# Three chained layers on one core: where TensorE's idle products write, how far they go on, and from which gap they are put in

## The chip, the cores and the metric

The kernel runs on one core of one Trainium2 chip. The metric is the device time of one execution in microseconds (us), lower is better. TensorE (PE) multiplies matrices, VectorE (DVE), ScalarE (ACT) and GpSimd (POOL) work on elements, SyncE (SP) issues most transfers. All five take their own instructions in order and wait for each other by semaphores.

## The reference, cut to what matters

Three layers follow each other. Everything is float32; 4 batches of 576 tokens, 512 columns.

```
attention: softmax(mask(q k^T / 8)) v         8 heads of 64, window of 64 tokens
channel mix: xk = mu_k x + (1-mu_k) x_prev ;  xr likewise with mu_r
             sigmoid(xr w_r) * (max(xk w_k, 0)^2 w_v)
gated conv:  (sigmoid(conv5(x)) * (x w_val)) w_out
```

## The kernel before, in words

The 2304 tokens are cut into a first block of 256 and four of 512. Of each block, attention is computed in four units of two heads (`unit`, units 0 to 3 are the first block, 4 to 7 the second). A unit's steps are: scores on PE (`qk`, L416; its masking products stand in L423 and L427, the products of q and k in L433), row maxima on DVE (`top`, L468 and the line before), exponentials on ACT (`exp`, L476), a division by the row sum on DVE (`norm`, L486), transposes on PE (`tp`, L491 to L497), a copy of the transposed weights to SBUF by ACT or DVE (`pt`, L503 to L505), the product with the values on PE (`pv`, L508 to L512), and a copy of its result into `xT` by DVE or ACT (`x`, L517 to L519). `xT` feeds the channel mix, whose first product is an `r` product (`r_tile`, L627 in the first block).

Which instruction stands where is a table written by hand (`SLOT`): each step has a number, and `Plan.run` issues the steps in that order. `Plan.run` also keeps a rough forecast of when each step can start. Where a PE step is forecast to start more than `WAIT` after the PE step ahead of it, `Plan.run` calls `fill`, which puts in idle products: 128x128 products of a zeroed tile (`warm`, part of `sgs`) whose result no one reads. Their number is the forecast gap divided by `PASS`.

PSUM has three users in the opening. `p0` holds the scores of units 0 to 3 (two buffers). `scores` holds those of the later units; before, the idle products write there, so they have to end when unit 4's scores are made. `at` has two banks: transposes write the first; in the first block the value product of a unit writes the first 256 columns of the second bank, which `x` then reads. The other 256 columns of that bank are not used in the first block.

```
if w[0] == "pe" and self.fill and t - free.get("pe", self.BEGIN) > self.WAIT:
    self.fill(t, int((t - max(free.get("pe", 0), self.WARM) - 250) // self.PASS))
```

Of the kernel before, what the change touches and what calls it, by code (L numbers as in the profile page):

```python
# [8 lines left out]
F32 = mybir.dt.float32  # L9
# [11 lines left out]
P = 128  # L21
# [3 lines left out]
TA = 256  # L25
HP = H // 2
NF = DM // P
NFF = DFF // P
GAP = TAPS - 1
TB = 512  # L30
# [143 lines left out]
class Plan:  # L174
# [2 lines left out]
    TO_PE = 110  # L177
    BEGIN, START, LAND = 740, 700, 1270
    RAMP, STALL = 3500, 1300
    WAIT, PASS, WARM = 700, 430, 900  # L180
    TABLE = 1280

    def __init__(self, **rings):
# [2 lines left out]
    def op(self, key, eng, ns, deps, fn, ring=None, table=None, moves=0):  # L186

        self.ops.append((key, ((eng, ns, fn),), deps, ring, table, moves))

    def any(self, key, deps, *ways):  # L190

        self.ops.append((key, ways, deps, None, None, 0))
# [45 lines left out]
def tile_kernel(ctx, tc, qkh, vh, mu, conv, w_k, w_v, w_r, w_val, w_out, out):  # L238
    nc = tc.nc
    f32 = lambda ap: ap.bitcast(F32)  # L240
    V, G, ACT, PE, DMA = nc.vector, nc.gpsimd, nc.scalar, nc.tensor, nc.sync
# [49 lines left out]
    pq = pas.enter_context(tc.tile_pool(name="pq", bufs=1, space=PSUM, side="right"))  # L291
    pa = pas.enter_context(tc.tile_pool(name="pa", bufs=1, space=PSUM, side="right"))
# [3 lines left out]
    Q = {}  # L296
# [4 lines left out]
    warm = sgs[:, 0, :P]  # L301
# [68 lines left out]
    A = {}  # L370
# [3 lines left out]
    def unit(u):  # L374

        t, hp = UNITS[u]
        t0, n = BLOCKS[t]
# [62 lines left out]
        scores = lambda: a["ps"].rearrange("p h (c j) -> p h c j", j=P)[:, :, :n2]  # L440
# [48 lines left out]
        at = lambda b: Q["at"][:, b]  # L489

        def tp():  # L491
            if "at" not in Q:
                Q["at"] = pa.tile([P, 2, TB], F32, tag="at", name="at")
            a["pt"] = tile_(mx, "pt", [P, 2, TB])
            for i in range(2 * n2):
                b, c = divmod(i, n2) if t else (0, i)
                PE.transpose(at(b)[:, c * P:(c + 1) * P], a["s"][:, i, :], ident)  # L497
        op(("tp", u), "pe", 176 * n2 + 2, [("norm", u), "ident", *back("pv", 1), *([("x", w) for w in range(HP)] if t == 1 else [])], tp,
           ring=("pa", ("pts", u)))
        for h in range(2 if t else 1):  # L500
            pts = lambda h=h: (a["pt"][:, h, :n], at(h)[:, :n]) if t else (a["pt"][:, :, :n], at(0).rearrange("p (h q) -> p h q", h=2))
            m = n if t else 2 * n
# [102 lines left out]
    Ps, Sg, Ss, Rk = {}, {}, {}, {}  # L605
# [425 lines left out]
    for i, (key, w, dst, nm) in enumerate(pieces):  # L1031
        m = nm * key[1]
        users[key] = []
        for e in range(nm // P):
            k = (dict(w_r="r", w_k="h", w_v="v")[key[0]], m // P + e)
# [109 lines left out]

    idle = {}

    def first_idle():  # L1150
        idle["ps"] = Q["scores"] = pq.tile([P, 2, TB], F32, tag="qk", name="scores")
    op("idle", "none", 0, ["warm"], first_idle)

    def fill(t, n):
        if any(k in Ps for k in [("r", 0, m) for m in range(NF)]) or HP in A and "ps" in A[HP] or n <= 0:
            return
        for _ in range(n):
            PE.matmul(idle["ps"][:, 0, :P], lhsT=warm, rhs=warm, start=True, stop=True)
    plan.fill = fill
    with tc.manual_schedule():  # L1160
        plan.run()
# [52 lines left out]
```

## Time and profile before

| | |
|---|---|
| Runs shown | 421.28, 422.95, 423.63 us; median 422.95 |
| The profiled execution: own time, span | 423.3 us, 421.5 us |
| PE busy | 410.9 us, 97% of the span |
| DVE, ACT, POOL busy | 351.9, 256.7, 22.5 us |
| Idle products | 11, on line L1158 |

A busy PE is counted from modelled ends of matmuls. A float32 product shows as two matmul records. The times below are from the span's start.

### The profile page before, as it was taken

Reading aid. Unit: us, or ns where it says so; the run is one execution under the profiler, and the core shown is the slowest. Engines: PE = TensorE matmul, PEld = TensorE weight load, DVE = VectorE, ACT = ScalarE, POOL = GpSimd, SP = SyncE. Lnnn points to the kernel's source line nnn. Section 1 sums busy time; section 2 is a strip of 40 time slices with the busy share of each in tenths; the row PEclk is TensorE's granted clock in tenths of the full one; section 3 lists DMA queues with packets and bytes.
Section 4 is the critical chain, followed back from the end, with each engine's and each line's share of the span. In section 5 each row is a group of like instructions: output and inputs, shape, how many; then the busy total and the mean of one; then the engine's idle time right before and its main releaser. Section 6 shows DMA issues by size and latency. Waiting matters only on the chain.

```text
span 421.5 us, 9145 instructions
## 1 busy us (share of the span) xinstructions
PE 410.9 (97%) x3746; PEld 354.8 (84%) x3746; DVE 351.9 (83%) x511; ACT 256.7 (61%) x585; POOL 22.5 (5%) x62
## 2 busy tenths in 40 slices
PE   8789999999999999999999999999999999999996
PEld 6578888888888888888888888888888899999996
DVE  3899998988989799458978996988584999999970
ACT  4899997789996175765334645154223284577721
POOL 2114101000002000000000000000000000001000
PEclk9899999999999999999999999999999999999999
DMA  8998925333432522072375434434997913616622
GB/s 306 407 366 320 381 64 166 104 117 104 131 113 98 208 103 77 2 286 89 116 261 210 137 157 155 161 152 153 343 427 286 400 69 114 225 35 155 176 86 112
DMA packets 24714, 77.69 MB, mean 184 GB/s; under 512 B 2528, under 2 KB 3296, under 8 KB 22624
## 3 DMA queue, kind: packets, MB, share of 16 engines
q1 hardware_dynamic: 23952, 74.74, 48.5%
q0 software_dynamic: 576, 2.36, 2.9%
q8 instruction: 29, 0.48, 0.4%
q14 instruction: 13, 0.11, 0.1%
q10 hardware_dynamic: 144, 0.00, 0.0%
HBM read 53.90 MB, written 20.84 MB: 177 GB/s over the span
## 4 chain that ended last, share of the span: by engine, by line
PE 83%; DVE 13%; issue 1%; ACT 1%; ACTq 0%; POOL 0%; DVEq 0%; POOLq 0%
PE h L603 21%; PE v L603 21%; PE r L603 10%; PE at L497 4%; PE ao L512 4%; PE scores L433 4%; PE v L627 3%; PE h L627 3%; PE out L979 3%; PE out2m L873 3%; DVE x L771 2%; DVE gq L771 2%; PE val3m L873 2%; PE r L627 2%; DVE early L914 1%; DVE xt L761 1%
## 5 line engine op out<-in xcount | busy, mean ns | idle before, releaser
L603 PE MATMUL h<-x,wk 128*128 128x512 f32 x384 | 90.7, 391 | 0.0
L603 PEld LDWEIGHTS h<-x,wk 128*128 128x128 f32 x384 | 71.5, 188 | 14.8
L603 PE MATMUL v<-sh,wv 128*128 128x512 f32 x256 | 81.1, 390 | 0.0
L603 PEld LDWEIGHTS v<-sh,wv 128*128 128x128 f32 x256 | 48.1, 188 | 10.0
L603 PE MATMUL v<-sl,wv 128*128 128x512 f32 x128 | 49.8, 389 | 0.0
L603 PE MATMUL r<-x,wr 128*128 128x512 f32 x192 | 45.4, 391 | 0.0
L603 PEld LDWEIGHTS r<-x,wr 128*128 128x128 f32 x192 | 35.7, 188 | 7.3
L804 DVE SCALAR_TENSOR_TENSOR early<-early,wc 128x576 f32<-128x576 f32 x48 | 38.2, 810 | 3.1 <-ACT early L802 2.7
L476 ACT ACTIVATE s<-s,m 128x128 f32<-128x128 f32 x96 | 37.2, 397 | 4.6 <-DVE m L465 4.6
L603 PEld LDWEIGHTS v<-sl,wv 128*128 128x128 f32 x128 | 24.0, 188 | 4.9
L504 ACT ACTIVATE pt<-at 128x512 f32<-128x512 f32 x28 | 16.4, 601 | 13.6 <-PE at L497 13.6
L654 ACT ACTIVATE rk<-h 128x512 f32<-128x512 f32 (+1 forms) x23 | 12.1, 538 | 17.9 <-PE h L603 15.8
L563 DVE SCALAR_TENSOR_TENSOR xm<-xT,omu,xm 128x512 f32<-128x512 f32 x32 | 22.5, 744 | 0.6 <-POOL xT L569 0.6
L684 DVE TENSOR_TENSOR sl<-rk,sh 128x1024 fp32r<-128x1024 f32 x16 | 19.4, 1219 | 3.9 <-ACT rk L682 3.8
L706 DVE TENSOR_TENSOR sgs<-v,sgs 128x512 f32<-128x512 f32 (+1 forms) x20 | 12.5, 632 | 10.9 <-PE v L603 10.9
L678 ACT ACTIVATE sh<-rk 128x1024 fp32r<-128x1024 f32 x16 | 16.9, 1055 | 6.8 <-DVE rk L656 6.7
L512 PEld LDWEIGHTS ao<-pt,vt 128*64 128x64 f32 x512 | 16.2, 138 | 5.5 <-issue 2.8
L586 DVE TENSOR_TENSOR x<-xm,x 128x1024 fp32r<-128x1024 f32 x16 | 19.4, 1219 | 1.2 <-ACT x L583 1.1
L486 DVE TENSOR_TENSOR s<-s,m 128x1024 f32<-128x1024 f32 x16 | 19.5, 1219 | 0.2
L768 ACT ACTIVATE x<-xt 128x576 fp32r<-128x576 f32 x15 | 10.0, 677 | 15.4 <-DVE xt L761 9.4
L476 ACT ACTIVATION_READ_ACCUMULATOR s<-s,m 128x1 f32 x96 | 18.8, 196 | 0.0
L512 PE MATMUL ao<-pt,vt 128*64 128x64 f32 x512 | 18.4, 225 | 0.0
(200 smaller groups left out, 857.5 us busy)
## 6 DMA issues: line engine op xcount, KB each, us to landing
qk<-qk SPq DMA_DIRECT2D x16, 544.0 KB, 5.2
vt<-vh SPq DMA_DIRECT2D x16, 512.0 KB, 4.9
xb<-x2d SPq DMA_DIRECT2D x4, 1152.0 KB, 7.2
out_t<-st SPq DMA_DIRECT2D x15, 288.0 KB, 2.8
x2d<-sgs SPq DMA_DIRECT2D x16, 256.0 KB, 3.5
w_out<-w SPq DMA_DIRECT2D x8, 512.0 KB, 3.5
w_val<-w SPq DMA_DIRECT2D x8, 448.0 KB, 4.5
wk<-w_val SPq DMA_DIRECT2D x2, 1792.0 KB, 11.8
```

Of the source, the lines that this page charges most:

```text
L433: PE.matmul(a["ps"][rows, h, o:o + W + HW], lhsT=a["q"][heads[h], c * HW:(c + 1) * HW], rhs=a["k"][heads[h], c * HW:c * HW + W + HW], star ...
L476: ACT.activation(out=s, in_=scores()[:, c // n2, c % n2, :] if by_pe else s, func=AF.Exp, scale=D ** -0.5 if by_pe else 1.0, bias=l(0)[:, ...
L486: lambda: V.tensor_tensor(out=a["s"], in0=a["s"], in1=l(1).unsqueeze(2).to_broadcast(sq), op=ALU.mult))
L512: PE.matmul(a["o"][heads[h], c * W:(c + 1) * W], lhsT=a["v"][:, c, heads[h]], rhs=a["pt"][:, h, c * W:(c + 1) * W], start=True, stop=True)
L563: V.scalar_tensor_tensor(out=m, in0=xT[:, f, :n], scalar=omu[:, c:c + 1], in1=m, op0=ALU.mult, op1=ALU.add)
L586: lambda E: E.tensor_tensor(out=dst(1), in0=src(), in1=f32(dst(0)), op=ALU.subtract))
L603: PE.matmul(ps, lhsT=a, rhs=b[:, kt, :], start=(kt == 0 and i == 0), stop=(kt == nk - 1 and i == 2))
L627: PE.matmul(Ps[key][:, :n], lhsT=ws(kt), rhs=x()[:, kt, :], start=kt == 0, stop=kt == nk - 1)
L678: ACT.activation(out=Ss[t][0][:, f, :n], in_=rk(), func=AF.Square)
L684: lambda E: E.tensor_tensor(out=Ss[t][1][:, f, :n], in0=rk(), in1=f32(Ss[t][0][:, f, :n]), op=ALU.subtract))
L804: V.scalar_tensor_tensor(out=o, in0=x, scalar=c, in1=o, op0=ALU.mult, op1=ALU.add)
L873: PE.matmul(z[bank][:, j, :HS], lhsT=lhs, rhs=rhs, start=new and kt == 0 and e == 0, stop=kt == 1 and e == 2, skip_group_check=not new)
```

## The change

The idle products get a new place to write, columns 256 to 383 of the second bank of `at`, which is therefore taken from its pool at the start. They no longer end with unit 4's scores: they go on until a unit of the second block has its transposes or an `r` product was issued, whichever is first. `WAIT` goes from 700 to 400 and `PASS` from 430 to 250, so shorter forecast gaps get idle products, and more of them. No row of the order table changes.

```diff
-    WAIT, PASS, WARM = 700, 430, 900
+    WAIT, PASS, WARM = 400, 250, 900
...
         def tp():
-            if "at" not in Q:
-                Q["at"] = pa.tile([P, 2, TB], F32, tag="at", name="at")
             a["pt"] = tile_(mx, "pt", [P, 2, TB])
...
-    idle = {}
-
     def first_idle():
-        idle["ps"] = Q["scores"] = pq.tile([P, 2, TB], F32, tag="qk", name="scores")
+        Q["scores"] = pq.tile([P, 2, TB], F32, tag="qk", name="scores")
+        Q["at"] = pa.tile([P, 2, TB], F32, tag="at", name="at")
...
     def fill(t, n):
-        if any(k in Ps for k in [("r", 0, m) for m in range(NF)]) or HP in A and "ps" in A[HP] or n <= 0:
+        if any(k in Ps for k in [("r", 0, m) for m in range(NF)]) or any("pt" in A[u] for u in A if u >= HP) or n <= 0:
             return
         for _ in range(n):
-            PE.matmul(idle["ps"][:, 0, :P], lhsT=warm, rhs=warm, start=True, stop=True)
+            PE.matmul(Q["at"][:, 1, TA:TA + P], lhsT=warm, rhs=warm, start=True, stop=True)
```

On PE, 11 idle products become 27: 6, 4 and 1 ahead of the first, third and fourth group of scores become 11, 6 and 2, and 1, 2, 3 and 2 are new, ahead of the first transposes and of the first, second and fourth value product. The other four engines issue the same instructions in the same order. In the changed kernel the idle products are on L1155, the transposes on L495, the value products on L510.

PE's first rows, before (`scores` and `qk_160` are PSUM tiles, `one` and `low` the masks that DVE makes):

```order
L1158 MATMUL scores<-sgs 128x128 [waits Pool_49]
L1158 MATMUL scores<-sgs 128x128 x5
L423 LDWEIGHTS one [waits DVE_49]
L423 MATMUL qk_160<-low,one 64x256
L427 LDWEIGHTS one
```

The same rows in the changed kernel:

```order
L1155 MATMUL at<-sgs 128x128 [waits Pool_49]
L1155 MATMUL at<-sgs 128x128 x10
L423 LDWEIGHTS one [waits DVE_49]
L423 MATMUL qk_166<-low,one 64x256
L427 LDWEIGHTS one
```

Five more idle products stand between the start and the first scores; nothing else moved there.

PE from the end of unit 4's scores to unit 2's transposes, before (`xm` and `sgs` on the right hold the weights and values of the first block, `pt_340` and `pt_379` are the transposed weights of units 0 and 1):

```order
L433 MATMUL scores<-qk_148 32x96 x31
L497 MATMUL at<-ident,xm 128x128 [waits DVE_49,Pool_49]
L497 MATMUL at<-ident,xm 128x128 x3
L512 MATMUL at<-pt_340,sgs 64x64 [waits DMAHW0_49,Activation_49]
L512 MATMUL at<-pt_340,sgs 64x64 x7
L497 MATMUL at<-ident,xm 128x128 [waits DVE_49]
L497 MATMUL at<-ident,xm 128x128 x3
L512 MATMUL at<-pt_379,sgs 64x64 [waits DMAHW4_49,DVE_49]
L512 MATMUL at<-pt_379,sgs 64x64 x7
L497 MATMUL at<-ident,xm 128x128 x4
```

The same stretch in the changed kernel:

```order
L433 MATMUL scores<-qk_149 32x96 x31
L1155 MATMUL at<-sgs 128x128
L495 MATMUL at<-ident,xm 128x128 [waits DVE_49,Pool_49]
L495 MATMUL at<-ident,xm 128x128 x3
L1155 MATMUL at<-sgs 128x128 [waits Activation_49]
L1155 MATMUL at<-sgs 128x128
L510 MATMUL at<-pt_349,sgs 64x64 [waits DMAHW0_49]
L510 MATMUL at<-pt_349,sgs 64x64 x7
L495 MATMUL at<-ident,xm 128x128 [waits DVE_49]
L495 MATMUL at<-ident,xm 128x128 x3
L1155 MATMUL at<-sgs 128x128 [waits DVE_49]
L1155 MATMUL at<-sgs 128x128 x2
```

One idle product without a wait of its own comes ahead of the first transposes. The two and the three ahead of the value products now carry the wait for ACT or DVE that the value product carried before; the value product behind them keeps the wait for its transfer alone. The two ahead of the fourth value product stand in the same way.

## Rows read from the trace of the kernel before

**Rows 1.** The page: PE's granted clock in 40 slices of the span.

```profile
PEclk9899999999999999999999999999999999999999
```

**Rows 2.** PE's waits over the span: waited for, us in total, times, longest.

```profile
PE at L512 <- DVE xT L518: 1.2, 1, 1.2
PE at L512 <- DVE pt L505: 1.2, 1, 1.2
...
PE val0m L873 <- ACT early L885: 0.7, 1, 0.7
...
PE at L512 <- ACT pt L504: 0.7, 1, 0.7
```

**Rows 3.** Timeline of PE, the opening: start, us, what [idle before <-releaser].

```profile
0.99 2.93 PE L1158 MATMUL scores<-sgs 128*128 128x128 f32 x12 [0.99 <-POOL sgs L302]
3.85 0.43 PE L423 MATMUL qk<-low,one 64*64 64x256 bf16 x4
...
4.26 0.89 PE L433 MATMUL qk<-early 64*32 64x96 f32 x32
...
5.49 0.74 PE L433 MATMUL qk<-early 64*32 64x96 f32 x32
6.16 1.16 PE L1158 MATMUL scores<-sgs 128*128 128x128 f32 x8
7.81 0.31 PE L423 MATMUL qk<-low,one 64*64 64x256 bf16 x4 [0.49 <-ACT xm L476]
...
8.07 0.56 PE L433 MATMUL qk<-early 64*32 64x96 f32 x32
8.56 0.49 PE L1158 MATMUL scores<-sgs 128*128 128x128 f32 x2
9.20 0.31 PE L423 MATMUL qk<-low,one 64*64 64x256 bf16 x4 [0.16 <-ACT xm L476]
```

**Rows 4.** Timeline of PE, from unit 4's scores to the first `r` product.

```profile
11.82 0.53 PE L433 MATMUL scores<-qk 64*32 64x96 f32 x21 [0.71 <-issue]
12.27 0.66 PE L497 MATMUL at<-ident,xm 128*128 128x128 f32 x4
13.62 0.69 PE L512 MATMUL at<-pt,sgs 128*64 128x64 f32 x16 [0.69 <-ACT pt L504]
...
16.07 1.05 PE L512 MATMUL at<-pt,sgs 128*64 128x64 f32 x16 [1.18 <-DVE pt L505]
17.05 1.12 PE L497 MATMUL at<-ident,xm 128*128 128x128 f32 x4
...
18.73 1.33 PE L433 MATMUL scores<-qk 64*32 64x96 f32 x64
...
22.46 0.69 PE L512 MATMUL at<-pt,rk 128*64 128x64 f32 x16 [1.20 <-DVE xT L518]
23.08 1.13 PE L627 MATMUL r<-x,words 128*128 128x256 f32 x4
```

**Rows 5.** Timeline of PE, scores of unit 6.

```profile
26.25 1.00 PE L433 MATMUL scores<-qk 64*32 64x96 f32 x64
```

**Rows 6.** Timeline of ACT: unit 0's first exponential, a copy of unit 1, a copy of unit 3.

```profile
6.25 0.37 ACT L476 ACTIVATE xm<-qk,first_m 128x128 f32<-128x128 f32 x1 [3.59 <-DVE first_m L468]
...
18.21 0.39 ACT L519 ACTIVATE xT<-at 128x256 f32<-128x256 f32 x1 [0.69 <-PE at L497]
...
21.35 0.60 ACT L504 ACTIVATE pt<-at 128x512 f32<-128x512 f32 x1 [0.44 <-PE at L497]
```

**Rows 7.** Timeline of DVE: the last piece of the masks.

```profile
2.99 0.16 DVE L320 CAST one<-ident 128x128 bf16<-128x128 f32 x1
```

**Rows 8.** The idle products' line: duration ns of one record, min/median/max.

```profile
L1158 PE MATMUL scores<-sgs x22: 275/421/582, 1.0 to 8.8; 128*128 128x128 f32 x22
```

**Rows 9.** Stretches: us, PE, PEld, DVE, ACT, POOL, PEclk, DMA share, GB/s.

```profile
12.93:16.07 3.14, 1.27 (x21) 0.97 (x21) 2.74 (x9) 3.10 (x11) 0.00 (x0) 1.00 1.03 405
17.00:18.00 1.00, 1.00 (x8) 0.72 (x4) 1.00 (x2) 0.52 (x4) 0.51 (x1) 0.50 1.01 420
```

## Prediction, made before the changed kernel ran

> **What bounds the kernel now.** I read the page first, for who is busy and how the clock runs. PE is the engine that is nearly always busy, and its clock is at the upper level (9 is the highest digit) everywhere but in the second of the 40 slices [rows 1]. PE's waits say where PE stands still: 1.2, 1.2 and 0.7 us ahead of the value products on L512, all before the first `r` product, and after it nothing longer than 0.7 us [rows 2]. From 23.08 us, where the first `r` product starts [rows 4], PE feeds itself to the end almost without a gap. So the start of that product decides: what the change moves there, it moves at the end, one for one. It touches nothing later.
>
> The opening is a chain through three engines. PE makes idle products from 0.99 us, then the first scores, whose last group of records ends at 4.26 + 0.89 = 5.15 [rows 3]. ACT, idle for 3.59 us, starts its exponentials at 6.25 [rows 6], and all that follows hangs on them. Further on, transposes (PE), a copy (ACT or DVE) and value products (PE) alternate, and PE stands ahead of each value product until the copy is done [rows 4].
>
> The clock column says 1.00 for the first microseconds, but the work says otherwise: a record of an idle product takes 421 ns in the middle of the list and 275 at best [rows 8], and the q-k records of a score group take 0.89, then 0.74, then 0.56 us [rows 3]. I read this as PE at the lower level until about 6 us, then at the upper one. A second low stretch is in the clock column itself, 0.50 between 17 and 18 us; ahead of it PE had worked 1.27 of 3.14 us [rows 9]. There the 16 records of a value product take 1.05 us instead of 0.69, four transposes 1.12 instead of 0.66 [rows 4].
>
> **The change, part by part.** The price of an idle product first. The twelve records of the first six last 2.93 us, the first alone 0.58, so the other eleven come every (2.93 - 0.58) / 11 = 0.214 us, 0.427 a product, at the low clock. Eight records last 1.16 us and two 0.49, so six more cost 0.67: 0.112 a record, 0.223 a product, at the high clock [rows 3, 8].
>
> Start, 11 products for 6. The masks are ready at 2.99 + 0.16 = 3.15 us [rows 7], and PE comes to the first scores at 3.85 without a gap [rows 3]: the idle products already end last there, so five more push the scores back by 5 x 0.427 = 2.13, to 5.98. What comes then runs at the high clock and takes what the third group takes, 8.07 + 0.56 - 7.81 = 0.82, and ends at 6.80 instead of 5.15. **Delay 1.65.** Bounds: 1.1 if the clock rises while the longer list still runs and the five cost the high price, 2.13 if it rises only after the first scores. I take 1.65, since the present rise, near 6 us, falls just at the new end of the list. ACT's exponentials come later by the same.
>
> Ahead of the third score group, 6 for 4: PE was idle for 0.49 there, waiting for an exponential that also comes later now [rows 3]; two more cost 0.45 and fit. **0**, up to 0.2 if they don't quite. Ahead of the fourth, 2 for 1: the gap was 0.16 [rows 3], the product costs 0.223. **0.06**, between 0 and 0.22.
>
> Ahead of the first transposes, one new product that waits for nothing: PE came there late, straight from unit 4's scores [rows 4]. **0.22**; 0 if the norm ends last there.
>
> Ahead of the first, second and fourth value product, 2, 3 and 2 new ones. The order says what they do: they write a tile that a copy reads, so the wait of the value product has moved to the first idle product ahead of it. PE stands still as long as before, until ACT or DVE is done, and only then makes the idle products, with the value product queued behind them. They lie on the path in full: 7 x 0.223 = **1.56**. Bounds: 0 if the value product's transfer ended last and they hid behind it, 7 x 0.427 = 2.99 at the low clock. Who waits for these products: the next transposes on PE itself, then the `pt` and `x` copies on ACT and DVE.
>
> Here the Trainium skill, page "PSUM — Partial Sum Buffer", section "PSUM bank collisions raise a hardware error", speaks against the change: PSUM is to be guarded by bank and quadrant, not by address, so columns that nobody uses in a bank that is being read are not free. By that rule the three and the last two have to wait, because the second bank is being read, but the first two don't, because the copy ahead of them reads the first bank; the late products would then be five, 1.12 us. In the order of the changed program all three groups carry a wait for ACT or DVE; no run here shows yet which of them costs.
>
> The 0.71 us gap in the middle of unit 4's scores waits for nothing that the profile shows [rows 4]. If something comes in by its own time there, a later PE waits less. Bounds 0 and -0.71; I take **-0.2**, nearer to 0, as the place may hold the gap and not the time.
>
> The low clock after 16 us. In the new order seven products lie between these gaps that PE did not have before, so I expect the clock to stay up. What it gives back on PE: 1.05 - 0.69 = 0.36 on the value product, 1.12 - 0.66 = 0.46 on the transposes [rows 4], 1.33 - 1.00 = 0.33 on the scores of unit 5 [rows 4, 5], 1.15 together. What can pass through: ACT waited 0.69 and 0.44 us for these transposes [rows 6], 1.13. I take **-1.1**, between 0 (it falls all the same) and -1.15.
>
> Other engines' instructions and queues are unchanged; they have the same work behind a later PE, which gives them more time. **0**.
>
> **Sum:** 1.65 + 0 + 0.06 + 0.22 + 1.56 - 0.2 - 1.1 = 2.19, say **+2.3**, since the 0 ahead of the third scores can only err upwards. The profiled execution's own time is 423.3 (span 421.5 and 1.8 around it), which lies 0.35 above the median of the runs, 422.95. 423.3 + 2.3 = 425.6; from the median 425.25. I forecast **425.3 us**.
>
> **The rivals.**
> *A, the clock falls all the same.* The gaps ahead of the copies stay as long as they were, because the idle products stand behind the wait and not in it; nothing in the rows shows that a little work between them is enough. Then -1.1 is gone, and some late products run at the low price: 423.3 + 2.19 + 1.1 = 426.6, up to 427.2. For it: PE had worked through much of the time before the fall and it came nevertheless [rows 9]. Chance 0.22.
> *B, not slower: the clock rises early in the list.* Place: the start. If the longer unbroken stream brings the high clock before 5 us, the five products cost 1.1 and the score groups behind them run fast from their first record; with the unexplained gap swallowed whole and the second fall gone it is 1.1 + 1.56 - 0.71 - 1.1 = 0.85: 424.1, or 423.8 from the median. It decides from a first-score delay of 1.1 or less. Against it: before, PE was as unbroken from 0.99 us on, and the clock came near 6 [rows 3]. The same time comes out if the opening is as I say and the late products hide behind the transfers: 2.19 - 1.56 = 0.6. Chance 0.22.
> In the Trainium skill, page "TensorE: Matmul & The Clock Gate", section "What's actually happening", the throttled state is the default and activity releases it. By that rule alone the added products could only help the clock; it is B's mechanism and the -1.1 of the forecast, and the low records at the start agree with it.
> *C, faster.* B's opening and free late products together: 0.85 - 1.56 = -0.7, 422.6, still no measurable gain. Beyond that I find no source: 0.03.
>
> **How the numbers follow.** A measurement of this kernel tells about 0.5% from no change, 2.1 us: above 425.06 is slower, below 420.84 faster. The forecast has 0.53, and its own range, 424.2 to 426.4, lies about two thirds above the line: 0.35 slower, 0.18 same. A gives 0.22 slower, B 0.22 same, C 0.03 faster: slower 0.57, same 0.40, faster 0.03. For 8 in 10 the range runs from 423.3, inside B, to 427.2, the upper end of A.
>
> **What would show it.** In the new profile: 22 records at the start, the first scores near 6.0 and ACT's first exponential near 7.9 us; idle products directly ahead of three value products, with PE's wait ended by ACT or DVE named at them; no low clock between 16 and 20 us; the first `r` product near 25.3. I am wrong if that product starts before 24 us, if the idle products lie inside the gaps, or if the time after it changes by more than 0.5 us.

## The result, and the profile after

The changed kernel takes 425.56 us (median of 7 executions, 424.99 to 426.3), the kernel before 422.06 (7 executions, 421.28 to 423.63; the three shown ahead are among them). The ratio is 1.0078, 95% interval 1.0059 to 1.0096: 3.5 us slower. The forecast of 425.3 and its range held, and so did its sign. The change itself was forecast as 2.35 us and measured as 3.5; the section on the prediction says by what luck the time came out right all the same.

The profiled execution has an own time of 425.44 us and a span of 423.7. Of the page, the line of PE's granted clock (before: [rows 1]):

```profile
PEclk9999999999999999999999999999999999999999
```

The low slice of before is gone. PE's waits (before: [rows 2]):

```profile
PE at L1155 <- DVE xT L516: 1.2, 1, 1.2
PE at L1155 <- DVE pt L503: 1.2, 1, 1.2
...
PE val0m L871 <- ACT early L883: 0.7, 1, 0.7
PE at L1155 <- ACT pt L502: 0.7, 1, 0.7
PE scores L433 <- issue: 0.4, 1, 0.4
PE qk L423 <- ACT xm L476: 0.4, 1, 0.4
```

The three waits of 1.2, 1.2 and 0.7 us are as long as they were, and they now stand at L1155, the idle products, instead of at the value products (L512 then, L510 now). The timeline of PE in the opening (before: [rows 3]):

```profile
0.99 4.69 PE L1155 MATMUL at<-sgs 128*128 128x128 f32 x22 [0.99 <-POOL sgs L302]
5.61 0.31 PE L423 MATMUL qk<-low,one 64*64 64x256 bf16 x4
...
5.87 0.56 PE L433 MATMUL qk<-early 64*32 64x96 f32 x32
...
7.11 1.60 PE L1155 MATMUL at<-sgs 128*128 128x128 f32 x12
9.09 0.31 PE L423 MATMUL qk<-low,one 64*64 64x256 bf16 x4 [0.37 <-ACT xm L476]
...
10.48 0.31 PE L423 MATMUL qk<-low,one 64*64 64x256 bf16 x4
```

There are 22 records at the start for 12, and the first scores begin at 5.61 for 3.85. Their q-k records take 0.56 us, which is the high clock, where before they took 0.89. ACT's first exponential (before: [rows 6]):

```profile
7.53 0.37 ACT L476 ACTIVATE xm<-qk,first_m 128x128 f32<-128x128 f32 x1 [4.87 <-DVE first_m L468]
```

It is 1.28 us later than before (6.25). PE from unit 4's scores to the first `r` product (before: [rows 4]):

```profile
12.58 0.74 PE L433 MATMUL scores<-qk 64*32 64x96 f32 x37 [0.43 <-issue]
13.24 0.49 PE L1155 MATMUL at<-sgs 128*128 128x128 f32 x2
13.57 0.60 PE L495 MATMUL at<-ident,xm 128*128 128x128 f32 x4
14.86 0.71 PE L1155 MATMUL at<-sgs 128*128 128x128 f32 x4 [0.69 <-ACT pt L502]
15.50 0.69 PE L510 MATMUL at<-pt,sgs 128*64 128x64 f32 x16
...
17.95 0.94 PE L1155 MATMUL at<-sgs 128*128 128x128 f32 x6 [1.18 <-DVE pt L503]
18.82 0.69 PE L510 MATMUL at<-pt,sgs 128*64 128x64 f32 x16
...
20.39 1.00 PE L433 MATMUL scores<-qk 64*32 64x96 f32 x64
...
23.83 0.71 PE L1155 MATMUL at<-sgs 128*128 128x128 f32 x4 [1.24 <-DVE xT L516]
24.47 0.69 PE L510 MATMUL at<-pt,rk 128*64 128x64 f32 x16
25.09 2.00 PE L625 MATMUL r<-x,words 128*128 128x256 f32 x8
```

Each late group begins only when its wait ends, and the value product comes 0.64, 0.87 and 0.64 us behind the group's start. The second group waits for DVE's `pt` copy, which reads the first bank, and not for the `x` copy of the second bank, which is done 0.6 us earlier. Timeline of DVE:

```profile
16.87 0.42 DVE L516 COPY xT<-at 128x256 f32<-128x256 f32 x1 [1.17 <-PE at L495]
17.21 0.68 DVE L503 COPY pt<-at 128x512 f32<-128x512 f32 x1
```

In the forecast's first reading everything depends on the first `r` product, and that holds: from its start to the own time there are 423.3 - 23.08 = 400.22 us before and 425.44 - 25.09 = 400.35 now. In all fourteen profiles of this study this rest lies between 400.1 and 400.5 us, so from here on the start of that product stands for the time of a kernel's profiled execution.

### The profile page after: what moved, and what is told of

Its sections match the earlier page's. It is cut to its first block, busy times and chain, and to the rows that moved or that the text cites. A ratio compares the mean times of both kernels' runs of the same rounds, so it can differ in the third digit from the quotient of the medians.

```text
span 423.7 us, 9206 instructions
## 1 busy us (share of the span) xinstructions
PE 413.6 (98%) x3778; PEld 357.9 (84%) x3778; DVE 351.9 (83%) x511; ACT 257.0 (61%) x585; POOL 21.8 (5%) x62
## 4 chain that ended last, share of the span: by engine, by line
PE 84%; DVE 12%; ACT 1%; issue 1%; ACTq 0%; POOL 0%; DVEq 0%; POOLq 0%
PE h L601 21%; PE v L601 21%; PE r L601 10%; PE ao L510 4%; PE at L495 4%; PE scores L433 3%; PE v L625 3%; PE h L625 3%; PE out L977 3%; PE out2m L871 3%; DVE x L769 2%; DVE gq L769 2%; PE val3m L871 2%; PE at L1155 2%; PE val0m L871 2%; PE r L625 2%
## 5 line engine op out<-in xcount | busy, mean ns | idle before, releaser
L510 PEld LDWEIGHTS ao<-pt,vt 128*64 128x64 f32 x512 | 16.2, 138 | 5.5 <-issue 2.8
L510 PE MATMUL ao<-pt,vt 128*64 128x64 f32 x512 | 18.4, 225 | 0.0
```

The source lines that it names most:

```text
L510: PE.matmul(a["o"][heads[h], c * W:(c + 1) * W], lhsT=a["v"][:, c, heads[h]], rhs=a["pt"][:, h, c * W:(c + 1) * W], start=True, stop=True)
```

## The experiments

All kernels below compute the whole reference and differ in idle products alone (those with bfloat16 products also zero a small tile for them on POOL). Their numbers stand in a table by step instead of coming from the forecast of the plan: (start, third score group, fourth score group) and, ahead of value products, (first, second, fourth). So the kernel before is 6, 4, 1. A "+x" is the median against that of the kernel before in the same set of runs (422.07 for the first four kernels, 35 executions; 422.32 for the next four, 11; 422.35 for the last four, 35). The ratio and its interval go by all executions of both kernels, so they do not give quite the same difference as the medians.

### The added products of the opening alone

```diff
+    IDLE = {('qk', 1): 11, ('qk', 2): 6, ('qk', 3): 2}
```

> The opening alone: 11, 6 and 2 idle products ahead of the first, third and fourth score group, none further on, so PE does the same as the kernel before from unit 4's scores on. Theory (the longer list delays the first scores, the rest of the loss is the products behind the waits): the first exponential on ACT starts near 7.5 us as in the changed kernel, against 6.25 before; the unexplained PE gap shrinks by about 0.3; the time lies 1.0 to 1.3 us above the kernel before. Rival (the opening is absorbed further on, all of the loss is the late products): within 0.4 us of the kernel before. Rival (the opening makes the whole loss): 3 us or more above.

Measured: 423.38 us (422.75 to 424.19), ratio 1.0022, interval 1.0000 to 1.0043: +1.31. Timeline of PE:

```profile
5.50 0.31 PE L423 MATMUL qk<-low,one 64*64 64x256 bf16 x4
...
12.31 0.73 PE L433 MATMUL scores<-qk 64*32 64x96 f32 x37 [0.28 <-issue]
...
22.56 1.99 PE L625 MATMUL r<-x,words 128*128 128x256 f32 x8
```

ACT's first exponential starts at 7.42 us here, 1.17 later than before. By the medians the opening is a third to two fifths of the whole loss; the interval reaches from nothing to half of it. The profiled execution has the lowest time of the twelve (422.75), and its first `r` product is only 0.72 us later than in the second profile of before shown below (22.56 for 21.84), because the stop in unit 4's scores is 0.28 us long in it and not 0.70.

### The late products alone

```diff
+    IDLE = {('qk', 1): 6, ('qk', 2): 4, ('qk', 3): 1, ('pv', 0): 2, ('pv', 1): 3, ('pv', 3): 2}
```

> The late products alone: 6, 4 and 1 at the start as before, and 2, 3 and 2 ahead of the first, second and fourth value product, in the shared tile. Theory: they run after the wait and cost 0.64 + 0.87 + 0.64 = 2.15 us on the path (the starts in the changed kernel's trace); the clock stays up through 20 us; the time lies 1.5 to 2.2 us above the kernel before. Rival (priced by the issue rate alone, 7 x 0.223 = 1.56, and a low clock saved in every execution): 0.5 us above. Rival (the clock falls all the same): 2.2 us or more above, with 0.50 in the clock column.

Measured: 424.16 us (423.5 to 426.52), ratio 1.0044, interval 1.0024 to 1.0065: +2.09. Timeline of PE:

```profile
13.89 0.71 PE L1158 MATMUL at<-sgs 128*128 128x128 f32 x4 [0.69 <-ACT pt L502]
14.54 0.69 PE L510 MATMUL at<-pt,sgs 128*64 128x64 f32 x16
...
16.99 0.94 PE L1158 MATMUL at<-sgs 128*128 128x128 f32 x6 [1.18 <-DVE pt L503]
17.86 0.69 PE L510 MATMUL at<-pt,sgs 128*64 128x64 f32 x16
```

The same waits of 0.69 and 1.18 us end at the idle products, and 0.65 and 0.87 us of idle products follow. The larger part of the loss is here. 1.31 + 2.09 = 3.4, beside 3.5 for the change as a whole.

### The same late products, written where nothing is read

Is it the seven products or their waits that cost? The pool of the second block's value products (`ao`) holds a PSUM bank that nothing uses this early. The late products write there; the opening stays at 6, 4, 1.

```diff
+        Q["spare"] = Q["po"].tile([P, TB], F32, tag="ao", name="spare")
...
+        o = Q["spare"][:, :P] if key[0] == "pv" else Q["at"][:, 1, TA:TA + P]
```

> As the run with the late products alone, but they write to the PSUM bank that the second block's value products use later, which nobody reads yet, so they wait for no copy. Theory (they cost because they stand behind the wait): the value products start as in the kernel before or up to 0.2 us later each, the clock stays up, and the time equals the better executions of the kernel before, 421.3 to 422.1. Rival (the products cost wherever they stand): 1.5 us or more above the kernel before. Rival (the clock was of no importance): within 0.3 us of the kernel before's median, and executions with a low stretch not slower than those without.

Measured: 422.61 us (422.36 to 423.56), ratio 1.0015, interval 0.9996 to 1.0034: +0.54 where the same products behind waits cost 2.09. Timeline of PE:

```profile
13.04 0.61 PE L1159 MATMUL spare<-sgs 128*128 128x128 f32 x4
13.89 0.69 PE L510 MATMUL at<-pt,sgs 128*64 128x64 f32 x16 [0.24 <-ACT pt L502]
...
16.35 0.69 PE L510 MATMUL at<-pt,sgs 128*64 128x64 f32 x16 [0.51 <-DVE pt L503]
...
18.13 1.41 PE L433 MATMUL scores<-qk 64*32 64x96 f32 x64
...
21.94 0.69 PE L510 MATMUL at<-pt,rk 128*64 128x64 f32 x16 [0.76 <-DVE xT L516]
22.55 1.99 PE L626 MATMUL r<-x,words 128*128 128x256 f32 x8
```

The products run at once, inside the gaps, and PE's waits shrink to 0.24, 0.51 and 0.76 us. From the first to the second value product there are 16.35 - 13.89 = 2.46 us, as before without any idle product (16.07 - 13.62 = 2.45 [rows 4]): they cost nothing there. So the waits are the price. The time expected was 421.3 to 422.1, and it is half a microsecond more. In the profile the first `r` product comes 0.71 us later than in the second profile of before (22.55 for 21.84), from two places: the stop in unit 4's scores is 0.98 us for 0.70, and the scores of unit 5 take 1.41 us for 1.00, with a stop of 0.33 us in them that waits for nothing shown (the last section comes back to it).

### The whole change, with its late products in the spare bank

The edit is that of the kernel above, made to the changed kernel: 11, 6, 2, one ahead of the first transposes, and 2, 3, 2 into the spare bank.

> The changed kernel with one thing undone: the products ahead of the value products write to the bank nobody reads, so they fall into the gap. Theory: the changed kernel's time less 2.15, near 423.4, and 1.0 to 1.5 above the kernel before, the opening alone being left. Rival (the opening makes the whole loss): near 425.5. Rival (the late products make the whole loss): at the kernel before's time, near 422.1.

Measured: 423.62 us (423.15 to 424.78), ratio 1.0038, interval 1.0019 to 1.0056: +1.55. That is 1.94 us less than the change as it was made, by the place of seven products alone; what stays is the opening.

### The kernel before, looked at once more

The forecast booked 1.1 us for the low clock after 16 us. This run is the kernel before, unchanged.

> The kernel before, looked at once more. In the five traces so far the time is the start of the first r product plus 400.2 us, and its executions spread from 421.2 to 423.3. Theory (the first profiled execution, 423.3, had a low stretch at 16 to 19.6 us that most executions don't have): this one, if it has no 0.50 stretch, starts the first r product near 21.9 and takes 421.3 to 422.4. Rival (every execution has the low stretch, and the first profile was no exception): a 0.50 stretch before 22 us, and a first r product near 23.

Measured: 422.06 us. Timeline of PE:

```profile
16.06 0.69 PE L512 MATMUL at<-pt,sgs 128*64 128x64 f32 x16 [1.18 <-DVE pt L505]
16.68 0.66 PE L497 MATMUL at<-ident,xm 128*128 128x128 f32 x4
...
17.83 1.00 PE L433 MATMUL scores<-qk 64*32 64x96 f32 x64
...
21.23 0.69 PE L512 MATMUL at<-pt,rk 128*64 128x64 f32 x16 [1.21 <-DVE xT L518]
21.84 1.99 PE L627 MATMUL r<-x,words 128*128 128x256 f32 x8
```

There is no low clock here: the value product takes 0.69, not 1.05 us, the scores 1.00, not 1.33 [rows 4]. The first five rows of the table below agree within 0.01 us in the two executions, and at the first `r` product they differ by 23.08 - 21.84 = 1.24. So the low stretch is an event of some executions and not of others.

How many have it can be read from the mean granted clock that is on record for each execution: it is 0.996 or less in the profiles with a low stretch in the middle and 0.998 or more in those without. Of the 35 executions of the kernel before in the first set, 7 have 0.996 or less; they take 423.02 to 426.16 us. The other 28 have a median of 421.82. In the other two sets it is 2 of 11 and 11 of 35, so 20 of 81 in all. All seven executions of the changed kernel have 0.998 or more. The change does take the low stretch away, but three executions of the kernel before in four have none.

With the second profile as the base, the loss can be read off step by step:

| start, us | before, first profile | before, second | after | after - second |
|---|---|---|---|---|
| first scores | 3.85 | 3.85 | 5.61 | 1.76 |
| third score group | 7.81 | 7.82 | 9.09 | 1.27 |
| first transposes | 12.27 | 12.27 | 13.57 | 1.30 |
| first value product | 13.62 | 13.61 | 15.50 | 1.89 |
| second value product | 16.07 | 16.06 | 18.82 | 2.76 |
| q-k products of unit 5's scores | 18.73 | 17.83 | 20.39 | 2.56 |
| fourth value product | 22.46 | 21.23 | 24.47 | 3.24 |
| first `r` product | 23.08 | 21.84 | 25.09 | 3.25 |

Ahead of the first transposes 1.3 us are lost; then each late group adds its step, 0.59, 0.87 and 0.68, and 0.20 come back ahead of unit 5's scores.

### Shorter idle products: fewer, longer records

A bfloat16 product of 128x512 shows as 2 records (a weight load and a matmul) where a float32 product shows as 4, and takes about as long. If PE's stop in unit 4's scores stands at a count of instructions, such a list moves it. First with the numbers of before (6, 4, 1), then with 4 at the start, then with 4 at the start and 2, 4, 4 such products in the spare bank:

```diff
+            PE.matmul(o.rearrange("p (c j) -> p c j", j=P), lhsT=zero[:, :P],
+                      rhs=zero[:, None, :P].to_broadcast([P, TB // P, P]), start=True, stop=True)
```

> The kernel before with each idle product made as one bf16 product of 128x512 instead of a float32 one of 128x128: the same 0.43 us at the low clock, but two records on PE (one weight load, one product) instead of four, 22 fewer in all; counts 6, 4 and 1, in the second bank of the shared tile. In all six traces PE's unexplained gap stands ahead of its 449th record, 0.5 to 1.2 us long, at 10.9 to 11.9 us, whatever the products. Theory (PE runs out of instructions there, and the gap is tied to the place in the list): the gap stands ahead of record 449 again, now 22 records further on in the work, and is 0.2 to 0.4 us shorter; the time is 0.2 to 0.5 us below the kernel before. Rival (tied to a time or a transfer): the gap stays at the same scores and ends at the same time; time as before.

> As the run with the short list, with 4 products at the start instead of 6. The masks are ready at 3.15 us and the first q-k input lands at 3.67. Theory (the opening is bound by the idle list, as with 11 products): the first scores' masking products start near 3.2 instead of 3.85, the q-k products near 3.75 instead of 4.26, and the time is 0.4 to 0.6 us below the run with 6. Rival (fewer products bring the high clock later, and the first score groups lose what the start gains): no difference, or more.

> As the run with 4 short products at the start, with 2, 4 and 4 more ahead of the first, second and fourth value product, in the bank nobody reads, 20 records. Theory: they fall into the gaps and keep the clock up in every execution, at no cost; the median as in the run with 4, the spread of the executions smaller. Rival (each adds 0.1 to 0.2 to the value product behind it and moves PE's next run-out into the scores of unit 5, as with the float32 products in the gap): 0.3 to 0.6 us above the run with 4.

Measured: 427.02 us (ratio 1.0112, interval 1.0096 to 1.0128), 426.01 (1.0068, 1.0042 to 1.0095) and 424.08 (1.0043, 1.0028 to 1.0059). All are slower than before. The first was expected 0.2 to 0.5 us below the kernel before and lies 4.7 above it. The second lies 1.0 below the first, where 0.4 to 0.6 was expected; the third lies 1.9 below the second, where no difference was. Timeline of PE and the clock line of the page, of the first:

```profile
10.15 0.91 PE L438 MATMUL scores<-qk 64*32 64x96 f32 x54
13.88 0.55 PE L438 MATMUL scores<-qk 64*32 64x96 f32 x10 [2.82 <-issue]
14.36 1.11 PE L500 MATMUL at<-ident,xm 128*128 128x128 f32 x4
...
26.92 1.35 PE L630 MATMUL r<-x,words 128*128 128x256 f32 x5
```

```profile
PEclk9689999999999999999999999999999999999999
```

The stop moved in place, as a count of instructions would have it (54 of the 64 records are done, 43 before), but it grew to 2.82 us, and the low clock followed it (0.50 from 13.78 to 24.02 us). All four executions of the first kernel have a mean clock of 0.988 or less, and four of the six of the second have 0.992 or less. In the third kernel the stop is 1.71 us:

```profile
13.34 0.37 PE L438 MATMUL scores<-qk 64*32 64x96 f32 x8 [1.71 <-issue]
```

The clock stayed up behind it in the profile, but not in every execution as was expected: three of the six have a mean clock of 0.994 to 0.996, and they are the three slowest (424.49 to 424.78). The executions lie within 1.4 us of each other (423.41 to 424.78); in the second kernel they spread over 3.5.

### One product less, and many small ones

The last four look for a version that beats both kernels: 5, 4, 1 in float32; then bfloat16 products of 128x128, four times as many as a float32 list of the same length: 24, 12, 4; 20, 12, 4; and 20, 12, 4 with 2, 4, 4 products of 128x512 in the spare bank.

```diff
+    IDLE = {('qk', 1): 20, ('qk', 2): 12, ('qk', 3): 4, ('pv', 0): 2, ('pv', 1): 4, ('pv', 3): 4}
```

> Before, with 5 idle products at the start instead of 6, everything else as before. If the list at the start is on the path one for one, the first scores come 0.43 us earlier (near 3.4) and the first r product up to 0.4 earlier: 0 to 0.4 us faster than before. If PE's stop ahead of its 449th record is set by the number of records ahead of it, there are 4 records fewer and the stop is 0.1 to 0.2 us longer, which leaves 0.2 to 0.3. Rival: the stop, or the later rise of the clock, takes all of it, and the time is that of before or longer.

> Before, with bfloat16 idle products of 128x128 (2 records each where a float32 product has 4): 24, 12 and 4 ahead of the first, third and fourth score group instead of 6, 4 and 1, so about the same PE time and some 36 records more ahead of the stop in unit 4's scores. If the stop is tied to the 449th record and is shorter where PE comes to it later with more records behind it, it is 0.2 to 0.5 us instead of 0.7 to 1.0, and the time 0.2 to 0.5 us below before. Rival: the stop depends on when PE gets there alone, is as long as before, and the time is the same.

> As the kernel with 24, 12 and 4 bfloat16 idle products, with 20 at the start: the first scores come 4 products, some 0.4 us, earlier. If the start is on the path one for one, 0.4 us below that kernel, 0.5 to 0.9 below before. Rival: the clock rises later or the stop grows by as much, and it is no faster than that kernel.

> As the kernel with 20, 12 and 4, and besides bfloat16 idle products of 128x512 (2, 4 and 4) ahead of the first, second and fourth value product, written to a PSUM bank that nothing reads then, so without a wait and inside PE's gaps. If these stay inside the gaps, no low clock after 14 us in any profile and a time within 0.3 us of that kernel, with less spread between executions. Rival: they end behind the copies, as in the changed kernel, and cost 0.2 us each group, 0.5 or more together.

| | us | ratio, 95% interval | first scores | stop | first `r` |
|---|---|---|---|---|---|
| 5, 4, 1 | 421.72 | 0.9995 (0.9979 to 1.0010) | 3.43 | 0.42 | 21.19 |
| 24, 12, 4 | 423.03 | 1.0011 (0.9993 to 1.0030) | 3.67 | 0.89 | 23.01 |
| 20, 12, 4 | 422.10 | 1.0002 (0.9978 to 1.0025) | 3.36 | 0.64 | 21.29 |
| 20, 12, 4, gaps filled | 422.25 | 0.9997 (0.9986 to 1.0008) | 3.36 | 0.92 | 21.80 |

None is faster than before by more than the measurement tells: no version here beats it. (With 5, 4, 1 the nine executions without a low stretch have a median of 421.60, and the 24 of the kernel before in the same set 422.05; that sorting was made afterwards and is not a verdict.) With one product less the first scores come 0.42 us earlier, as expected, and the stop shrank instead of growing. With 24 small products the stop is 0.89, not 0.2 to 0.5: a longer list of short records did not shorten it, and that expectation fell. With 20 the time is 0.9 below that with 24, twice what was expected of the four products, but it is that of before and not 0.5 to 0.9 below. Eight of the twelve executions with 24 have a low stretch by their mean clock, and five of the twelve with 20. The profile with 24 shows the low clock again, at the place of [rows 4]; its timeline of PE:

```profile
16.05 0.97 PE L515 MATMUL at<-pt,sgs 128*64 128x64 f32 x16 [1.18 <-DVE pt L508]
16.95 1.12 PE L500 MATMUL at<-ident,xm 128*128 128x128 f32 x4
...
18.63 1.36 PE L438 MATMUL scores<-qk 64*32 64x96 f32 x64
```

The last kernel fills the gaps. Timeline of PE:

```profile
13.26 0.69 PE L515 MATMUL at<-pt,sgs 128*64 128x64 f32 x16 [0.26 <-ACT pt L507]
...
15.71 0.69 PE L515 MATMUL at<-pt,sgs 128*64 128x64 f32 x16 [0.32 <-DVE pt L508]
...
17.48 1.30 PE L438 MATMUL scores<-qk 64*32 64x96 f32 x64
```

The gaps are filled, and the value products are no later for it: there are 2.45 us from the first to the second (15.71 - 13.26), as before. Eleven executions lie between 421.9 and 422.51 us, none with a low stretch by its mean clock (a twelfth took 1428.7 us and is left out of the comparison; no profile shows what it met). The kernel before spread from 421.3 to 424.76 in the same set, 11 of its 35 executions with a low stretch. So filling the gaps takes the long executions away, and the short ones too: the stop is 0.92 us, and unit 5's scores take 1.30 for 1.00.

## Why the prediction was right, and where it was not

**What bounds.** Right: the time follows the first `r` product one for one, and nothing behind it moved.

**Start, forecast 1.65, measured 1.28** (ACT's first exponential at 7.53 for 6.25). The mechanism was right: the first score group takes the 0.82 us that were forecast (5.61 to 6.43). The size was high because the granted clock reached the upper level at 5.15 us, inside the list, so that the last two of the eleven products took the price of the high clock and the first scores came 1.76 us later, not 2.13. The third and the fourth group start 1.28 us late as well (9.09 for 7.81, 10.48 for 9.20 [rows 3]): 0 for both, as forecast for the third; the fourth's 0.06 was 0.

**One product ahead of the first transposes, forecast 0.22, measured 0.33** (13.24 to 13.57).

**Seven late products, forecast 1.56, measured 0.64 + 0.87 + 0.64 = 2.15** in the profile and 2.09 in the runs with these products alone. The mechanism was right, and the kernel with the spare bank shows it: without the wait the same products cost nothing between two value products. The term was mis-sized: the forecast priced the records alone, 0.223 us a product, and each group takes 0.2 us more than its records. That is the size of one weight load of such a product (line L1159 of the kernel with the late products in the spare bank, from the answer on that tile; ns, min/median/max):

```profile
L1159 PEld LDWEIGHTS spare<-sgs x14: 190/192/192, 12.9 to 20.8; 128*128 128x128 f32 x14
```

Whether it is that load which no longer hides was not tried.

All three groups waited, the first two products too: 0.69 us for ACT's copy, though that copy reads the other bank of the tile. Written to another tile, they ran beside the same copy at 13.04 us without a wait. I read this as a wait that the program sets for the tile as a whole. The Trainium skill, page "PSUM — Partial Sum Buffer", section "PSUM bank collisions raise a hardware error", speaks of banks; by its rule, as weighed in the prediction, the first two would have gone ahead, for 1.12 us together, and the trace does not agree with that. The prediction also said that the three have to wait because the second bank is being read. That reading was wrong: they waited for the `pt` copy of the first bank, until 17.95 us, and `x` had read the second by 17.29. Only the last two end their wait with `x`. No run here wrote into a bank that was being read, so on that it stays untested.

**The unexplained gap, forecast -0.2, measured -0.28** (0.43 for 0.71 us). The direction is borne out, the size is partly chance: the same opening with 11 products gave 0.28, 0.43 and 0.65 us in three kernels, the one with 6 float32 products 0.70, 0.71, 0.98 and 0.98.

**The low clock, forecast -1.1.** Measured between the profiles, it is gone and was worth 1.24. But the second profile of before does not have it either, so most of the time the change has nothing to gain there. This is the step that failed: "which lies 0.35 above the median of the runs". The forecast took the profiled execution as one like the others, and it was one of the quarter with a low stretch. Against a profile with one, the forecast was near: the first `r` product came 2.01 us later (25.09 for 23.08), for a sum of 2.19. Against the typical execution the effect of the change is 1.31 + 2.09 and a little for the transposes, 3.5 us, and not 2.35. That the forecast time came out near all the same is luck: the median of the three runs shown, 422.95, lay 0.9 above that of the seven, 422.06, and so the base carried most of what the term took off.

**Rivals.** A fell: the granted clock is at the upper level from 5.15 to 421.58 us, and no execution of the changed kernel has a mean below 0.998. B needed a first-score delay of 1.1 or less, which was 1.76, or late products that hide; they hide only in a bank that nothing reads. C fell with both.

## What to carry to other kernels

Filler that writes into a tile which a copy reads takes over the wait of the work behind it, and then runs in full on the path: see in the order where the wait has moved, or give the filler a tile of its own. Filler ahead of the first real work costs its own length there: here 1.76 us for five products, of which a faster first group gave 0.48 back. Before a gain is booked for removing an event in a profile, look whether the other executions have it: in the spread of their times, and for the clock in each execution's mean granted clock.

## What the runs showed of the hardware that was not expected

**A stop at one count of instructions.** The 0.71 us gap of [rows 4] that waits for nothing shown stands, in all fourteen profiles, directly behind PE's first 449 records (weight loads, matmuls and two of the sequencer, counted from the start), whichever instruction comes next. The expectations, which put it ahead of the 449th record, count one too few; nothing hangs on that. The stop ends 2.26 to 2.49 us after the first packet of the DMA queue of kind "instruction" starts. From the traces, in us (the starts of the packet and of the two records):

```
                                packet   449th    450th   450th - packet
before, first profile            9.34    10.87    11.82    2.48
before, second                   9.56    10.87    11.81    2.26
after                           10.23    11.90    12.58    2.35
6, 4, 1 of 2 records each       11.60    10.82    13.88    2.28
4, 4, 1 of 2 records each       11.22    10.62    13.61    2.39
24, 12, 4 of 2 records each      9.20    10.43    11.57    2.37
5, 4, 1                          8.68    10.40    11.06    2.37
```

I read this as PE running out of loaded instructions until the next block has come; the profile has no row that says so. Two more numbers fit it: a second such stop, in unit 5's scores, stands 256 records further on in the two traces that have it (the late float32 products in the spare bank, and the last kernel), and the page counts 29 packets with 0.48 MB in that queue, 16 KB each. What starts the first packet is open. In all fourteen traces it starts 3.3 to 4.0 us after PE's 176th record, which itself starts between 5.32 and 7.71 us; the number 176 was picked from the traces as the one with the least scatter, so this is a link and not a shown cause. It would explain why the short lists lost: with fewer records early on, the 176th comes later (7.63 us with 6, 4, 1 of 2 records each, 5.98 before), while PE gets to the 449th no later.

**The clock does not rise at the same time in the same opening.** With 11 products at the start the granted clock reached the upper level at 4.18, 4.91 and 5.15 us (three kernels, the same instructions until then), with 6 float32 products at 5.55, 5.95, 6.29 and 6.37. These are the starts of the first clock record of each trace; in the changed kernel the idle records ahead of it take 421 ns and those behind it 275. The forecast had taken one such time as fixed. The Trainium skill, page "TensorE: Matmul & The Clock Gate", section "What's actually happening", says that the number of slow products differs from run to run of one kernel; these traces agree.

**The low stretch after 16 us comes and goes.** Of the profiles without filler in the later gaps and with a stop under 1 us, two have it (before, first profile; 24, 12, 4) and four do not; of the six with filler there, none has. The mean clocks show that this is not a rule for every execution: of the kernels with filler in the later gaps, the one with the late products alone has a low stretch in 1 of 12 executions and the third of the short lists in 3 of 6, the other four in none of 42. Nor is it the filler alone: the longer opening by itself has none in 12. What decides is open.
